# Two attention cores of a fused attention and convolution kernel, each issued from one written-out order: the even value rows first and interleaved with the last logit products, the odd value projections later

## The chip, the cores and the metric

The kernel runs on one core of one Trainium2 chip. The metric is the device time of one execution in microseconds (us). Before the change it was 421.42 us, the median of 3 runs (420.72 to 423.65). Engines are named as in the profile: PE is TensorE (PEld its weight loads), DVE is VectorE, ACT is ScalarE, POOL is GpSimd, SP is SyncE, which only issues transfers.

## What is computed

Two layers alternate, A, B, A, B, with the same weights both times. A is a layer norm, an attention over 8 earlier positions two apart, an output projection and a residual. B is a layer norm, a long convolution with a kernel K that depends on the weights alone, and a residual. There are 2048 positions, 512 channels and 32 heads of 16.

```python
def _A_ref(x, wqkv, wo):
    H = 32; Dh = D // H
    W, dil = 8, 2
    q, k, v = ...                       # x @ wqkv, by heads
    idx = pos[:, None] - (jnp.arange(W) * dil)[None, :]
    mask = idx >= 0
    logits = jnp.einsum("bhsd,bhswd->bhsw", q, kg) * scale      # kg, vg: k, v gathered at idx
    attn = _softmax(jnp.where(mask, logits, -1e9), axis=-1)
    o = jnp.einsum("bhsw,bhswd->bhsd", attn, vg)
    return o @ wo
def _B_ref(u, A_re, ...):
    K = jnp.einsum("dn,dnl,dn->dl", Cc, P, dB).real
    y = irfft(rfft(u) * rfft(K))        # padded to twice the length, along positions
    return y + u * Dskip
x = x + _A_ref(_layernorm(x), wqkv, wo)
x = x + _B_ref(_layernorm(x), ...)      # and both once more
```

## The kernel before, in words

**Layout and stages.** A position is 16 p + a: p is the partition (128), a the "row" (16 rows). A step of two positions back is a step of two rows back at the same p, and, where it leaves the 16 rows, the row 16 further on of the partition before. So keys (`kT_ext`) and values (`v_ext`) are stored with 14 extra rows in front, which are the last 14 rows moved by one partition. For values that move is done by DMA. The even extra rows come from the even rows only and the odd from the odd. All data stays in on-chip memory, in bf16, between the layers.

The program goes through five stages: making K and the front of attention 0 (normalize, transpose, keys, queries), attention core 0, the transform of layer B with the front of attention 1 after it, attention core 1, and the second transform. Only the two attention cores, which are one function, `LayerA.core`, are touched.

**What an attention core does.** It has 4 blocks q of 4 rows, and 4 feature groups ft of 128 channels.

- Logit products, `mult(q, ft)` (L295, DVE): queries times the 8 shifted keys, 128x4096. The result, `prod`, has 2 buffers. `lsum(q, ft)` (L302, PE) sums it over the channels of a head with 32 small matmuls into the PSUM tile L of the block (2 buffers); at ft = 3 the mask is added (L285).
- Softmax of a block: `mx` (L365, DVE, the maximum), `sub_exp` (L372 on PE subtracts it, L375 on ACT is the exponential), `recip` (L382 on PE sums, L384 and L386 on ACT make the reciprocal as the exponential of minus a logarithm), `norm_p` (L392, DVE, the weights `attn`).
- Projections on PE, each copied out by ACT: queries of a block, `q_proj` (L185, copy L187, 2 buffers of `qT`), values of a row, `v_proj` (L351, copy L353). When row 14 is done, two DMAs on SP's queue move the even rows into the extra ones (L356, L357), and the load of `wo` follows in core 0; with row 15 the odd ones go. In core 0 the loads of x into `x_sb` (L1359) hang on the same two places.
- Value rows: `pv_mult` (L402, DVE, 128x4096, `pav` with 2 buffers), `pv_sum` (L412, PE, 64 matmuls; its PSUM tile `po` has 1 buffer; ACT copies it to `oT`, L415), `out_proj` (L422 and L424, PE; L430 on ACT evicts it into `x_sb` with the row's sum, L108 takes the sum of squares; rows 12 to 15 use L428).
- Layer norm for the next layer, by blocks of four rows: `u_begin` (L133, L135, L140 on DVE and then a power on POOL, L141, or two ACT steps, L118 and L119), `u_end` (L148, DVE), `u_apply` (L160, DVE, for odd rows, L158, ACT, for even rows). `x_stats` (L101, DVE) is for the last rows.

**What sets the order.** Each of DVE, ACT, PE and SP runs its instructions in the order in which the program issues them. Nothing is moved by a planner in these stages. In `core` that order comes from loops. The first goes over the logit products of blocks 0 to 2; between them a list of projections is dealt out evenly (`per`, `acc`): the queries of block 1 (in core 1 only; in core 0 they are done earlier), six value rows, the queries of block 2, and the other value rows, even rows ahead of odd ones. What is left of the list is issued after the loop. The second loop goes over the 16 value rows in the order 0, 2, 1, 3, 4 and so on, and has the four logit products of block 3 at its steps 1, 3, 5 and 7.

```python
projs += [(v_proj, a) for a in vs[:6]] + [(q_proj, 2, ft) for ft in range(NDT)]
projs += [(v_proj, a) for a in vs[6:]]
...
proj(100)
linit(3)
q_proj(3, 0)
rows = [0, 2, 1, *range(3, NA)]
for n in range(16):
    pv_mult(rows[n])
```

**Hooks.** Other work hangs on steps of these loops by a dictionary of events. In core 0 it is the making of a table g2 for the transform (indices on POOL, four sines on ACT, L700, each followed by a store to `g_dram` on SP, L701), the reading back of K (`k_half_load`, 18 DMAs for each half into `k_rl`, L1264 and L1280), the fix of its first element (`k_half_fix`, L1350, DVE), and eight copies of K into `k_perm` (`k_part`, L1354; even ones on ACT, odd ones on DVE). The sines use the memory of `k_perm` as scratch, so the first copy of K has to wait until the stores of g2 have read it. The table load for the logarithm and exponential and the load of the transform's weights (`load_w2`, L560) are hooked in too. In core 1 the rest of the front's key and query projections is hooked to the first products.

**After the cores.** The transform stages issue from written orders of their own and begin with a PE pass (L756) over the normalized rows, whose results DVE and ACT cast (L745). They are not changed.

Of the kernel before, what the change touches and what calls it, by code (L numbers as in the profile page):

```python
# [20 lines left out]
P = 128  # L21
S = 2048
# [4 lines left out]
NA = 16  # L27
NDT = 4
# [35 lines left out]
u m UA m u m u m u m u u yD yA u m yA m m u u u m yA m yA  # L64
yA m yD yD yA yD yA yA yA yD z01D z03D yA yA z00D z02D z12D z11A z10D z13B
"""

def build_a_consts(tc, nc, cpool, tpool):
    c = {}
# [93 lines left out]
class LayerA:  # L163
# [140 lines left out]
        if ft == NDT - 1:  # L304
            self.mask(q)

    def core(self, x_sb, u, lnp, ev=None, nprod=0):

        tc, nc, lnst, l = self.tc, self.nc, self.lnst, self.layer
        ident, nident = self.c["ident"], self.c["nident"]  # L310
        scale = float(DH) ** -0.5
        xnT = self.xnT
        ev = ev or {}
        if self.ps_l is None:
            self.open_logits()
        st, linit, mult, lsum = self.st, self.linit, self.mult, self.lsum

        def event(key):
            for f in ev.get(key, ()):
                f()  # L320

        with ExitStack() as c2:
            big = c2.enter_context(tc.tile_pool(name=f"a{l}_big", bufs=1, reuse_waits="tile"))
# [24 lines left out]
            def v_proj(a):  # L348
                pp = pq_tile()
                for dt in range(NDT):  # L350
                    nc.tensor.matmul(pp[:], lhsT=xnT[:, dt, a * P:(a + 1) * P],  # L351
                                     rhs=wv[:, dt, :], start=(dt == 0), stop=(dt == NDT - 1))
                nc.scalar.copy(v[:, 14 + a, :].rearrange("p (d h) -> p d h", h=H), pp[:].rearrange("p (h d) -> p d h", h=H))  # L353
                if a >= 14:
                    b = a - 14
                    nc.sync.dma_start(v[1:113, b:14:2, :], v[0:112, 16 + b:30:2, :])  # L356
                    nc.sync.dma_start(v[113:128, b:14:2, :], v[112:127, 16 + b:30:2, :])  # L357
                    if b + l == 0:
                        self.load_wo(big)
                    event(("v", b))  # L360

            def mx(q):
                L = st[q]["L"]
# [88 lines left out]
            def u_apply(a0, rows, eng=None):  # L452
                rstd, nb = lns[a0]
                for a in rows:
# [2 lines left out]

            nc.sync.dma_start(v[0:1, 0:14, :].rearrange("p a (n c) -> p (a n) c", c=64),
                              self.c["zrow"].unsqueeze(1).to_broadcast([1, 112, 64]))
            projs = [(q_proj, 1, ft) for ft in range(NDT)] if 1 not in self.qT else []  # L460
            vs = [*range(0, NA, 2), *range(1, NA, 2)]
            projs += [(v_proj, a) for a in vs[:6]] + [(q_proj, 2, ft) for ft in range(NDT)]
            projs += [(v_proj, a) for a in vs[6:]]
            slots = [(0, ft) for ft in range(nprod, NDT)] + [(q, ft) for q in (1, 2) for ft in range(NDT)]
            free = 2 if l else 0
            lead = 0 if l else 2
            per, acc = (len(projs) - lead) / (len(slots) - free - 0.5), float(lead)

            def proj(n):
                nonlocal acc  # L470
                acc += n
                while acc >= 1 and projs:
                    f, *args = projs.pop(0)
                    f(*args)
                    acc -= 1

            for q, ft in slots:
                if q == 1 and ft == 0 and 1 not in self.qT:
                    while 1 not in self.qT or projs[0][0] is q_proj:
                        proj(1)  # L480
                event(("m", q, ft))
                mult(q, ft)
                event(("q", q, ft))
                if ft == 0:
                    linit(q)
                if q or ft >= free:
                    proj(per)
                if ft == 0 and q > 0:
                    mx(q - 1)
                lsum(q, ft)  # L490
                if ft == 0 and q > 0:
                    proj(0.5)
                    acc -= 0.5
                    sub_exp(q - 1)
                if ft == 2 and q > 0:
                    recip(q - 1)
                if ft == 3 and q > 0:
                    norm_p(q - 1)
            proj(100)
            linit(3)  # L500
            q_proj(3, 0)
            rows = [0, 2, 1, *range(3, NA)]
            for n in range(16):
                pv_mult(rows[n])
                if n in (0, 8):
                    mx(2 + n // 8)
                if n in (2, 10):
                    recip(2 + n // 8)
                if n in (4, 11):
                    norm_p(2 + n // 8)  # L510
                if n in (1, 3, 5, 7):
                    mult(3, n // 2)
                if n in (7, 11, 15):
                    u_begin(n - 7, n - 3, "act", "act" if n > 7 else "pool")
                if n in (8, 12):
                    u_end(n - 8)
                if n in (9, 10, 13, 14):
                    b0 = 0 if n < 11 else 4
                    r0 = b0 + (0 if n in (9, 13) else 2)
                    u_apply(b0, range(r0, r0 + 2))  # L520
                if n == 15:
                    x_stats(12)
                event(("p", n))
                if n in (1, 3, 5):
                    q_proj(3, n // 2 + 1)
                pv_sum(rows[n])
                if n in (0, 8):
                    sub_exp(2 + n // 8)
                if n == 15:
                    x_stats(13)  # L530
                    if l == 1:
                        u_end(8)
                        u_apply(8, range(8, 12), "dve")
                if n > 0:
                    out_proj(rows[n - 1])
                if n in (1, 3, 5, 7):
                    lsum(3, n // 2)
                event(("o", n))
            if l == 0:
                out_proj(15)  # L540
                return {"a": lambda: [u_end(8), u_apply(8, range(8, 12), "pool")], "s": lambda: x_stats(14), "t": lambda: x_stats(15),
# [744 lines left out]
def kernel(  # L1286
# [16 lines left out]
    nc = tc.nc  # L1303
# [57 lines left out]
    with tc.tile_pool(name="ctmp_g2", bufs=1) as g2tmp, tc.manual_schedule(engines=MAN):  # L1361
        gx, gs = build_g2(nc, g2tmp, C["p21"], g2_dram, kp[:].rearrange("p q a r -> p (q a r)"))
        G = lambda f, h: lambda: f(h)
        K = lambda h, j: lambda: k_part(h, j)
        ev = {("v", 0): [lambda: x_load((0,))], ("v", 1): [lambda: x_load((1, 2, 3))], ("o", 1): [lambda: k_half_load(0)], ("o", 2): [G(gs, 0)], 
              ("m", 0, 3): [G(gx, h) for h in range(4)],
              ("p", 3): [G(gs, 1)], ("p", 4): [G(gs, 2)], ("p", 5): [G(gs, 3), lambda: k_half_load(1)], ("o", 5): [lambda: nc.scalar.preload_act_table_set(EXP_LN)],
              ("p", 6): [lambda: k_half_fix(0), K(0, 0)], ("p", 7): [K(0, 1)], ("p", 8): [lambda: la.load_w2(w2_dram), K(0, 2)], ("p", 9): [K(0, 3)],
              ("p", 12): [lambda: k_half_fix(1), K(1, 0)], ("p", 13): [K(1, 1), K(1, 2)], ("p", 14): [K(1, 3)]}
        late = la.core(x_sb, u, lnp, ev, 3)  # L1370
    late["m"] = C["masks"]
    krctx2.close()
    la.close_logits()
# [13 lines left out]
    with tc.manual_schedule(engines=MAN):  # L1387
# [33 lines left out]
        fb.c_ps.close()  # L1421
        fb.c_grp.close()
        krctx.close()
        ev = {("p", 8): [lambda: la.load_w2(w2_dram)]}
        ev["m", 0, 0] = [last(("P", 3, 0), ("P", 3, 1), ("x", 0), ("x", 2), ("P", 3, 2), ("Q", 0, 1), ("e", 0), ("Q", 0, 2))]
        ev["m", 0, 1] = [last(("e", 1), ("e", 2))]
        ev["m", 0, 2] = [last(("e", 3))]
        ev["q", 0, 0] = [last(("P", 3, 3), ("Q", 0, 3))]
        la.core(x_sb, u, lnp, ev)
    la.close_logits()  # L1430

    fb = FftB(tc, nc, C, consts["ident"], w2_dram, g2_dram, kf_dram, x_sb, 1)
# [47 lines left out]
```

## Time and profile before

| what | value |
|---|---|
| median of 3 runs (lowest, highest) | 421.42 us (420.72, 423.65) |
| the profiled execution's own time | 418.89 us |
| its span, and the mean TensorE clock | 417.1 us, 0.991 |
| busy PE, PEld, DVE, ACT, POOL in the span | 320.5, 231.5, 387.9, 321.7, 37.7 us |
| making K, front of attention 0 | 0 to 114.8 us |
| core 0: logit half, value half | 114.8 to 139.9, 139.9 to 196.7 us |
| transform 0, front of attention 1 | 196.7 to 251.0, 251.0 to 276.1 us |
| core 1: logit half, value half | 276.1 to 312.3, 312.3 to 369.4 us |
| transform 1 | 369.4 to 417.0 us |

The stages overlap at their edges; the cuts are where DVE or PE goes over to the next. How to read it: a number in a "busy" column is the time in which the engine worked, and the stretch's length minus it is the time in which it waited. In a timeline a line is the start in us, the duration, engine, source line, operation, output and inputs with their shapes, and in brackets the idle time before it and what ended that. An "x3" after a line counts the operations that the line stands for. Lines are those of the kernel before unless said otherwise. SPq is SP's queue: its rows show the issue of a DMA, and the data land later.

### The profile page before, as it was taken

Reading aid. Unit: us, or ns where it says so; the run is one execution under the profiler, and the core shown is the slowest. Engines: PE = TensorE matmul, PEld = TensorE weight load, DVE = VectorE, ACT = ScalarE, POOL = GpSimd, SP = SyncE. Lnnn points to the kernel's source line nnn. Section 1 sums busy time; section 2 is a strip of 40 time slices with the busy share of each in tenths; the row PEclk is TensorE's granted clock in tenths of the full one; section 3 lists DMA queues with packets and bytes.
Section 4 is the critical chain, followed back from the end, with each engine's and each line's share of the span. In section 5 each row is a group of like instructions: output and inputs, shape, how many; then the busy total and the mean of one; then the engine's idle time right before and its main releaser. Section 6 shows DMA issues by size and latency. Waiting matters only on the chain.

```text
span 417.1 us, 15864 instructions
## 1 busy us (share of the span) xinstructions
PE 320.5 (77%) x7048; PEld 231.5 (55%) x7106; DVE 387.9 (93%) x515; ACT 321.7 (77%) x552; POOL 37.7 (9%) x46
## 2 busy tenths in 40 slices
PE   3000068999999987778998779999998978896885
PEld 2000036667756565556887768555665655566774
DVE  8999999999899999996999969979779999989995
ACT  6999998987445569987999998863555758779972
POOL 3000200000396000000500000000000020000000
PEclk9999998999999999999999999999999999999899
DMA  8940642113014666393226597730043027504506
GB/s 222 383 125 13 73 90 71 33 40 89 14 40 123 179 180 189 99 389 109 70 89 229 217 306 218 231 99 2 3 114 89 5 79 328 156 3 140 168 10 197
DMA packets 62462, 54.36 MB, mean 130 GB/s; under 512 B 33877, under 2 KB 50874, under 8 KB 61114
## 3 DMA queue, kind: packets, MB, share of 16 engines
q1 hardware_dynamic: 62250, 53.22, 42.0%
q8 instruction: 55, 0.90, 0.9%
q10 hardware_dynamic: 144, 0.13, 0.1%
q14 instruction: 13, 0.11, 0.1%
HBM read 30.28 MB, written 13.24 MB: 104 GB/s over the span
## 4 chain that ended last, share of the span: by engine, by line
PE 35%; DVE 21%; ACT 14%; issue 5%; DMA 5%; SPq 3%; DVEq 0%; ACTq 0%
PE pq L351 6%; DVE pav L402 5%; DVE t L805 5%; PE L L302 4%; DVE a1s L745 4%; PE pk L1175 4%; PE pq L185 3%; DVE prod L295 3%; PE pp L242 3%; PE po L412 3%; PE pp L1113 3%; PE pq L424 2%; SPq L1280 2%; DMA w_sb<-w_dram 2%; ACT ub L818 1%
## 5 line engine op out<-in xcount | busy, mean ns | idle before, releaser
L402 DVE TENSOR_TENSOR pav<-attn,v_ext 128x4096 bf16<-128x4096 bf16 x32 | 72.8, 2283 | 0.1
L295 DVE TENSOR_TENSOR prod<-qT,kT_ext 128x4096 bf16<-128x4096 bf16 x29 | 66.0, 2299 | 3.9 <-PE L L302 3.8
L412 PE MATMUL po<-ident,pav 64*128 64x64 bf16 x2048 | 36.3, 190 | 15.1 <-DVE pav L402 7.7
L412 PEld LDWEIGHTS <-pav 64*128 64x128 bf16 x2048 | 32.5, 95 | 26.0 <-DVE pav L402 14.9
L1103 PE MATMUL pt<-ident,x_blk 128*128 128x128 bf16 x64 | 7.0, 260 | 43.4 <-ACT x_blk L158 43.4
L1015 DVE TENSOR_TENSOR A_t<-A_t,pow_t 128x1024 bf16<-128x1024 bf16 (+4 forms) x46 | 38.1, 868 | 0.2
L424 PE MATMUL pq<-wop,oT 128*128 128x512 bf16 x121 | 31.7, 379 | 4.3 <-issue 3.8
L353 ACT CAST v_ext<-pq 128x512 bf16<-128x512 f32 x32 | 18.8, 587 | 19.2 <-PE pq L351 17.5
L818 ACT CAST ub<-pb 128x1024 bf16<-128x1024 f32 x32 | 32.2, 1036 | 1.7 <-DVE t L805 0.8
L763 PE MATMUL pb<-a1s,w_sb 128*128 128x64 bf16 x768 | 28.4, 196 | 6.2 <-ACT a1s L745 2.9
L302 PEld LDWEIGHTS <-prod 128*128 128x128 bf16 x928 | 27.0, 96 | 8.1 <-DVE prod L295 2.5
L1103 PEld LDWEIGHTS <-x_blk 128*128 128x128 bf16 x64 | 5.4, 117 | 46.1 <-ACT x_blk L158 44.4
L745 DVE CAST a1s<-pb 128x1024 bf16<-128x1024 f32 x23 | 27.0, 1215 | 3.9 <-PE pb L756 3.9
L763 PEld LDWEIGHTS <-w_sb 128*128 128x128 bf16 x768 | 25.8, 100 | 8.6 <-issue 6.8
L351 PE MATMUL pq<-wv,xnT 128*128 128x512 bf16 x118 | 29.9, 379 | 0.5
L1113 PE MATMUL pp<-xnT,kT_ext 128*128 128x512 bf16 x87 | 25.0, 406 | 6.2 <-ACT qT L1118 3.3
L302 PE MATMUL L<-ind,prod 128*128 128x8 bf16 x928 | 27.4, 166 | 0.8 <-DVE prod L295 0.6
L415 ACT CAST oT<-po 128x512 bf16<-128x512 f32 x32 | 18.5, 577 | 11.5 <-PE po L412 11.2
L745 ACT CAST a1s<-pb 128x1024 bf16<-128x1024 f32 x25 | 24.9, 1034 | 2.5 <-PE pb L756 2.2
L1175 PEld LDWEIGHTS <-A_t 128*64 128x64 bf16 (+1 forms) x512 | 22.3, 105 | 3.6
L1175 PE MATMUL pk<-B_t,A_t 128*64 128x84 bf16 (+1 forms) x512 | 24.1, 203 | 0.1
L832 PE MATMUL pb<-Wp,t 64*128 64x64 bf16 x512 | 19.4, 192 | 5.9 <-ACT ub L818 2.8
(225 smaller groups left out, 809.8 us busy)
## 6 DMA issues: line engine op xcount, KB each, us to landing
w_sb<-w_dram SPq DMA_DIRECT2D x8, 1024.0 KB, 9.4
w_dram<-w_zero SPq DMA_DIRECT2D x1, 4096.0 KB, 14.8
kf_ring<-kf_dram SPq DMA_DIRECT2D x13, 256.0 KB, 3.7
kf_ring<-kf_dram SPq DMA_DIRECT2D x26, 128.0 KB, 3.6
v_ext<-v_ext SPq DMA_DIRECT2D x4, 784.0 KB, 6.2
x_blk<-in_A_x_dram SPq DMA_DIRECT2D x4, 512.0 KB, 4.1
kT_ext<-in_A_wqkv_dram SPq DMA_DIRECT2D x4, 512.0 KB, 10.1
x_sb<-in_A_x_dram SPq DMA_DIRECT2D x4, 512.0 KB, 5.4
```

Of the source, the lines that this page charges most:

```text
L295: nc.vector.tensor_tensor(pr, self.qT[q][:, ft].unsqueeze(1).to_broadcast([P, W, 4, P]), kap, ALU.mult)
L302: self.nc.tensor.matmul(L[:, al, w, ft * 8:(ft + 1) * 8], lhsT=pr[:, w, al, :], rhs=self.c["ind8"][:], start=(ft == 0 and w == 0 and al % ...
L351: nc.tensor.matmul(pp[:], lhsT=xnT[:, dt, a * P:(a + 1) * P], rhs=wv[:, dt, :], start=(dt == 0), stop=(dt == NDT - 1))
L402: nc.vector.tensor_tensor(pv[:], attn[:, n % 4].unsqueeze(2).to_broadcast([P, W, DH, H]), vap, ALU.mult)
L412: nc.tensor.matmul(po[:, h, 0, ft, :], lhsT=pvf[rows, w, ft * P:(ft + 1) * P], rhs=ident[rows, rows], start=(w == 0 and ft == 0), stop=(w ...
L424: nc.tensor.matmul(pw[:], lhsT=oT[:, ftp, :], rhs=self.wo[:, ftp, :], start=False, stop=(ftp == NDT - 1))
L745: (self.nc.scalar.copy if eng == "act" else self.nc.vector.tensor_copy)(dst, src)
L763: nc.tensor.matmul(p2[:, j, :], lhsT=self.w2[:, ec * EC + j, :], rhs=a1s[:, ec * EC + j, :], start=True, stop=True)
L818: nc.scalar.copy(ub[:], p2)
L1015: return lambda: nc.vector.tensor_tensor(*args)
L1113: nc.tensor.matmul(pps[kind, b, ft][:], lhsT=la.wqk[:, dt, c:c + P], rhs=la.xnT[:, dt, b * 512:(b + 1) * 512], start=(dt == 0), stop=(dt = ...
L1175: nc.tensor.matmul(o, lhsT=lhs, rhs=Bt[:, ri, c * CH + ql].rearrange("p b g -> p (b g)"), start=(not half and j % 4 == 0 and ri == 0), sto ...
```

## The change

Both cores now get a string, one letter for each step, and `core` only walks through it. The letters are m for `mult`, l for `lsum`, q for `q_proj`, v for `v_proj`, x for `mx`, e for `sub_exp`, r for `recip`, n for `norm_p`, P for `pv_mult`, S for `pv_sum`, O for `out_proj`, t for `x_stats`, b, d and a for `u_begin`, `u_end` and `u_apply` (now one row each). Digits and other capitals are the hooks. In core 0, 0 makes the indices of g2, 1 and 6 read back the halves of K, 2 to 5 are the sines with their stores, 7 is the table load, w the weights' load, 8 and 9 are the fixes, A to H the copies of K. In core 1, 0 to 3 are the rest of the front.

Every step of before is still there, once. What differs is the order:

- The value rows go 2, 0, 4, 6, 3, 1, 5, 8, ... in core 0 and 0, 4, 6, 1, 2, 3, 5, 10, ... in core 1. The four logit products of block 3 stand behind 2, 4, 6 and 8 value products, as before (in core 1 behind 2, 3, 6 and 8).
- The projections have places of their own instead of an even spread: even value rows still come ahead of odd ones, and that of row 15 comes after the last logit sum of block 2.
- The steps of softmax and layer norm and the hooks have other neighbours. An output projection can stand ahead of the value sum that it followed, and the row's normalizing is split by rows.

```diff
+CORE0 = """
+vm0vvvlmxvqlqmeqmlvrlvvmmlqvvnmxlvevmlvmrlvvlvnPxqSeqPSm1OlPr2SPq3mOSlPOPSn4OSmq56O7lP8ASOPOmbBS
+lPxCdwSeOPOaSaraPSODPanSbPOd9ESOaaPFSOPHOaSPGbtSOta
+"""
+CORE1 = """
+0mvl12ml3mqmqqqlqlmvxvevlrvmlmvlqmqmlnxqvvvvlevvmmllrmvvvlvnqPxeSPmqSlPrOSOqmPqSOPOlSPmnSlOPPSmO
+SObwPldxOSeaOPaSPraaPSOnbSOPdSaOPSOPaSaaOPbttSdaaaOa
+"""
+ROWS0 = (2, 0, 4, 6, 3, 1, 5, 8, 7, 9, 11, 10, 13, 12, 14, 15)
+ROWS1 = (0, 4, 6, 1, 2, 3, 5, 10, 7, 8, 9, 11, 12, 13, 14, 15)
+VROWS = (*range(0, 16, 2), *range(1, 16, 2))
...
-    def core(self, x_sb, u, lnp, ev=None, nprod=0):
+    def core(self, x_sb, u, lnp, order, ev, nprod=0):
...
-                    event(("v", b))
+                    if ("v", b) in ev:
+                        ev["v", b]()
...
-            for q, ft in slots:
...
-            for n in range(16):
-                pv_mult(rows[n])
...
+            qft = [(q, ft) for q in range(4) for ft in range(NDT)]
+            blocks = [(q,) for q in range(4)]
+            rows = [(a,) for a in (ROWS1 if l else ROWS0)]
+            ops = dict(
+                m=calls(mult, *qft[nprod:]), l=calls(logit(lsum), *qft[nprod:]),
+                q=calls(q_proj, *qft[len(self.qT) * NDT:]), v=calls(v_proj, *((a,) for a in VROWS)),
+                x=calls(mx, *blocks), e=calls(sub_exp, *blocks), r=calls(recip, *blocks), n=calls(norm_p, *blocks),
+                P=calls(pv_mult, *rows), S=calls(pv_sum, *rows), O=calls(out_proj, *rows[:15]), t=calls(x_stats, (12,), (13,)),
+                b=calls(u_begin, (0, 4, "act", "pool"), (4, 8, "act", "act"), (8, 12, "act", "act")),
+                d=calls(u_end, (0,), (4,), (8,)),
+                a=calls(u_apply, *((a0, (a,)) for a0 in (0, 4) for a in range(a0, a0 + 4)), *((8, (a,), "dve") for a in range(8, 12))))
+            ops = {key: iter(f) for key, f in ops.items()}
+            for c in "".join(order.split()):
+                if c in ev:
+                    ev[c]()
+                else:
+                    next(ops[c])()
...
-        late = la.core(x_sb, u, lnp, ev, 3)
+              "0": lambda: [gx(h) for h in range(4)], "1": lambda: k_half_load(0), "6": lambda: k_half_load(1),
+              "2": G(gs, 0), "3": G(gs, 1), "4": G(gs, 2), "5": G(gs, 3),
+              "7": lambda: nc.scalar.preload_act_table_set(EXP_LN), "w": lambda: la.load_w2(w2_dram),
+              "8": lambda: k_half_fix(0), "9": lambda: k_half_fix(1)}
+        ev |= {c: K(i // 4, i % 4) for i, c in enumerate("ABCDEFGH")}
+        late = la.core(x_sb, u, lnp, CORE0, ev, 3)
...
-        la.core(x_sb, u, lnp, ev)
+        la.core(x_sb, u, lnp, CORE1, ev)
```

## The prediction, made before the changed kernel was run

> **What bounds the kernel now.** The page came first: it says which engine has no room left.
>
> ```profile
> PE 320.5 (77%) x7048; PEld 231.5 (55%) x7106; DVE 387.9 (93%) x515; ACT 321.7 (77%) x552; POOL 37.7 (9%) x46
> ```
>
> DVE is busy 387.9 of 417.1 us, so an order can only win idle DVE time. The view by stretches says where it is; its columns are the stretch, its length, then PE, PEld, DVE, ACT busy.
>
> ```profile
> 114.80:139.90 25.10, 24.19 (x348) 14.78 (x350) 23.94 (x13) 12.67 (x23) 17.25 (x11) 1.00 0.40 103
> 139.90:169.60 29.70, 23.88 (x694) 16.61 (x700) 29.32 (x21) 23.39 (x47) 0.51 (x1) 1.00 0.57 165
> ...
> 276.10:312.30 36.20, 35.73 (x483) 21.53 (x490) 31.04 (x19) 19.51 (x35) 0.00 (x0) 1.00 0.13 35
> 312.30:340.90 28.60, 24.57 (x708) 16.92 (x716) 28.53 (x18) 17.46 (x42) 0.00 (x0) 1.00 0.13 35
> ```
>
> Rows 1 and 3 are the logit halves of the two attention cores. PE is full there (35.73 of 36.20), while DVE lacks 5.1 us in core 1 and 1.2 in core 0. Rows 2 and 4 are the starts of the value halves: DVE full, PE with 4 to 6 us of room. DVE's timeline names its waits in core 1:
>
> ```profile
> 288.47 1.23 DVE L365 TENSOR_REDUCE mx<-L 128x128 bf16<-128x1024 f32 x1 [0.61 <-PE L L285]
> 289.61 4.48 DVE L295 TENSOR_TENSOR prod<-qT,kT_ext 128x4096 bf16<-128x4096 bf16 x2
> 294.96 2.29 DVE L295 TENSOR_TENSOR prod<-qT,kT_ext 128x4096 bf16<-128x4096 bf16 x1 [0.87 <-PE L L302]
> 298.55 0.69 DVE L392 TENSOR_TENSOR attn<-ex,rs 128x1024 bf16<-128x1024 bf16 x1 [1.29 <-ACT rs L386]
> ```
>
> The last one ends after a chain: logit sums, sum of exponentials on PE, two ACT steps, then the attention weights. It comes again at 311.69.
>
> Third, SyncE's timeline, as nothing on it may be late:
>
> ```profile
> 140.99 0.64 SPq L356 DMA_DIRECT2D v_ext<-v_ext  x1
> ...
> 142.62 4.42 SPq L1359 DMA_DIRECT2D x_sb<-in_A_x_dram  x3
> 147.09 0.61 SPq L1264 DMA_DIRECT2D k_rl<-kd_dram  x1
> 147.74 12.15 SPq L1280 DMA_DIRECT2D k_rl<-kd_dram  x17
> 159.99 3.83 SPq L701 DMA_DIRECT2D g_dram<-k_perm  x4
> ```
>
> From 140.99, when the last value projection (row 15) is copied out, the queue runs without a pause to the stores of g2 at 159.99. The tile view of g_dram gives 5.1 us from issue to landing: the first store lands at 165.1. ScalarE's first copy into that memory (L1354) starts at 166.90.
>
> [...] the trace agrees that all products cost alike (2.28 us, one each 2.20 us), so no order makes one cheaper. [...]
>
> ```profile
> 169.09 1.02 POOL L141 TENSOR_TENSOR ln_rstd<-ln_rstd,ln_mh 128x4 f32<-128x4 f32 x1 [37.05 <-DVE ln_rstd L140]
> ...
> 341.19 2.89 POOL L141 TENSOR_TENSOR ln_rstd<-ln_rstd,ln_mh 128x4 f32<-128x4 f32 x1 [96.59 <-DVE ln_rstd L140]
> ```
>
> It is the same power on 128x4. In core 0 it began before a value product and took 1.02; in core 1 a product was running from 340.92 to 343.20, and it ended at 344.08, 0.9 after that.
>
> **The change part by part.** Nothing is removed or added: all products, projections, sums, copies and DMAs are the same, and each queue's DMAs keep their order. What moves is worked out by lanes, with one instruction's pitch: logit product or value product 2.20 (DVE), maximum 1.13, attention weights 0.60; projection 0.87, logit sum 0.80, value sum 1.04, output projection 1.08 (PE); projection copy 0.48, row statistics with eviction 1.36, K copy 0.95 (ACT).
>
> *Core 0, logit half.* From 114.87 on DVE has 9 products (19.8), 2 maxima (2.3) and 2 weights (1.2) before the first value product: 138.2 if it never waits. It now starts at 139.91. The new order puts each weights step behind the next product, so the waits of 0.37 and 0.72 and the small ones between products go: lead 1.7. PE's sum doesn't change: from 118.56, 16 projections, 8 logit sums and 2.3 for the rest are 22.6, so 141.2, as now (the next projection, q3, starts at 141.30). So DVE leads only where PE has room later, and it has (row 2). But the projection of row 15 now stands behind the last logit sum and mask, 1.0 us later on PE; its copy ends at 141.8 instead of 140.97, and everything queued behind it on SyncE moves by 0.8: the odd shift, the three x_sb loads, 18 loads of k_rl, the g2 stores. The shift itself is safe: the new row order needs odd rows first after four even ones, at about 152.6, and it lands at about 148.5.
>
> *Core 0, value half.* DVE runs on: 8 value products, 4 logit products, a maximum, a weights step and the K fix are 28.3, so 166.5, when the first layer-norm block (L133) is due; now it starts at 168.47. This lead is given back. ScalarE reaches its first K copy at about 163.4 (now 165.6 before its table load), but the first g2 store lands at 165.1 + 0.8 = 165.9. Behind that copy stand, in ScalarE's order, the evictions of rows 5 and 1, and the block needs row 1's statistics: 165.9 + 0.95 + 0.48 + 1.36 = 168.7. Row 1 was long done before; this is a new wait of about 2 us on DVE. With 0.2 for the last scalars and 0.6 for the K copy behind them the next value product starts at about 169.8; now 169.56. From there DVE has 22.0 us to the end of its last one (now 22.3; one apply of 0.33 has moved behind): 191.8 against 191.9.
>
> *Core 0, end.* Now an output projection stands ahead of the last value sum, which starts 0.85 after its product. In the new order it is done before, and the first 16 K transform matmuls (L756) stand ahead too. So value sum 191.9 to 193.0, copy to 193.6, two output projections to 195.1; now 196.05. The transform stage starts 0.95 earlier and keeps it: ScalarE (52.79 of 54.30) and DVE (50.27) are full in it. Core 0: minus 1.0.
>
> *Core 1, logit half.* PE is full in both orders. Walking both lanes: the first product of block 1 now waits for a logit sum behind three more projections (287.1, about 1.3 idle), two further products wait 1.3 and 0.8, but both weights steps (1.29 each) are covered. The first value product starts at 310.7; now 312.30. Lead 1.6. It needs the even shift, which landed at 309.99 and whose projection keeps its place on PE: 0.7 of slack. PE's first value sum stays at about 315.0 (now 314.65), and its room in row 4 carries the lead.
>
> *Core 1, value half.* The layer-norm block comes at 338.9 (now 340.46). It now has one value product behind it before its result is read, where product and maximum stood before. The power on GpSimd [...] ends 0.9 later, as in the row above; DVE then stands for about 0.9 and the maximum is late with it. Bounds: 0 if the power slips in ahead, 1.0. I take 0.9. The end is as now, 0.7 earlier. Later transfers follow: the w2 load waits for the last logit product and moves with it.
>
> Sum: 1.0 + 0.7 = 1.7; I round up to 2.0, since the first DVE cast of the transform gains more than PE does (now idle for 2.56 before it). The profiled run took 418.89 around its span of 417.1; the median shown is 421.42, and the difference applies to it: 419.4.
>
> **Rivals.**
> 1. *Both leads kept.* ScalarE isn't held at the K copy (if the k_rl loads run faster than the sum says) and the power slips in. Then core 0 gives 2.8 (P-sums end at 190.1) and core 1 1.6: 4.4, so 417.0. For: DVE has no other wait in the value halves. Against: the queue has no pause in which to catch up.
> 2. *Hidden.* The leads arrive and the transform stages don't pass them on, as they wait for transfers or for GpSimd's applies (POOL, 198.20 to 204.94): 421.4. For: ScalarE and DVE share that stage, and it has a store chain of its own (L791, L808). Against: those transfers start from the same casts.
> 3. *Slower.* The wait at the K copy is longer than the lead: each us by which row 15's copy is later than 0.8 holds ScalarE, then row 1's statistics, then DVE, one for one. It decides from 0.8 + 2.0 = 2.8 us on; at 5 us the time is 423.6. For: PE in this stretch has under 1 us of room, so any hitch lands on the row 15 projection, last in its line. Against: the same matmuls in sum.
> That the change does nothing is out: the order on each engine differs.
>
> **How the numbers follow.** Forecast 0.45 (418 to 421), rival 1 0.20, rival 2 0.20, rival 3 0.15. The range 416.2 to 423.6 leaves out the ends of rivals 1 and 3. About 1% (4.2 us) is what a measurement can tell from no change. Faster by over 1% (under 417.2) takes most of rival 1 and a little of the forecast: 0.18. Slower by over 1% (over 425.6): 0.07, of rival 3. The rest, 0.75, is within 1%.
>
> **What would show it.** Right: first value product of core 0 near 138.2; SyncE's odd shift near 141.8; about 2 us of DVE idle before L133 or L135 of core 0 that ACT ends; about 0.9 before L148 of core 1 that POOL ends; core 1's weights steps without a wait. Wrong: no wait at L133 (rival 1), new DVE idle in the transforms (rival 2), a shift after 143 (rival 3).

## The result and the profile after

The changed kernel took 421.86 us (median of 20 runs, 417.47 to 423.92), the kernel before 421.42 (20 runs, 419.21 to 424.05). The ratio is 1.0006 with a 95% interval of 0.9982 to 1.0030, that is +0.3 us (-0.8 to +1.3): no difference that can be measured. The ratios of all runs here leave out executions over 1.5% above the fastest of their kernel (five of 22 for the later K copy below, at most three in any other set). The profiled execution took 420.96 us around a span of 419.2.

Lines of the changed kernel: L308 logit product, L401 weights, L411 value product, L421 value sum, L431 and L433 output projection, L439 and L121 eviction and sum of squares, L146 and L148 layer-norm block, L154 POOL's power, L161 scalars, L364 shift, L374 maximum, L1222 and L1238 loads of K, L1312 copies of K, L659 stores of g2, L703 casts of the transform, L790 its later matmuls. Times are us.

| mark | before | predicted | after |
|---|---|---|---|
| core 0: first value product | 139.91 | 138.2 | 139.15 |
| SyncE: odd shift | 140.99 | 141.8 | 142.74 |
| value product behind the layer-norm block | 169.56 | 169.8 | 170.50 |
| end of the last value product | 191.9 | 191.8 | 193.0 |
| last output projection done | 196.05 | 195.1 | 197.8 |
| tenth DVE cast of transform 0 into `a1s` | 209.91 | | 211.13 |
| core 1: first logit product | 276.15 | | 279.24 |
| from it to the first value product | 36.15 | 34.55 | 34.56 |
| from it to the first cast of transform 1 | 93.31 | 92.6 | 92.30 |
| span | 417.1 | 415.1 | 419.2 |

So the span's 2.1 is +1.2 up to transform 0, +1.9 in it and in the front behind it, and -1.0 in core 1. The view by stretches of the changed kernel (stretch, length, PE, PEld, DVE, ACT, POOL busy):

```profile
114.80:139.90 25.10, 23.88 (x348) 14.47 (x347) 24.95 (x14) 12.08 (x22) 19.25 (x11) 1.00 0.41 103
139.90:169.60 29.70, 25.32 (x644) 15.95 (x642) 27.95 (x17) 23.76 (x47) 0.00 (x0) 0.99 0.57 163
276.10:312.30 36.20, 36.20 (x492) 21.63 (x491) 31.61 (x23) 19.53 (x35) 0.00 (x0) 1.00 0.18 47
312.30:340.90 28.60, 26.91 (x714) 17.43 (x712) 28.60 (x16) 18.20 (x43) 0.00 (x0) 1.00 0.13 36
```

In core 0 DVE's waits have moved: 0.15 left in the logit half (1.2 before), 1.75 in the start of the value half (0.4 before). DVE's timeline there, and ScalarE's:

```profile
165.50 2.27 DVE L308 TENSOR_TENSOR prod<-qT,kT_ext 128x4096 bf16<-128x4096 bf16 x1
168.90 0.16 DVE L146 SCALAR_TENSOR_TENSOR ln_msq<-ln_s 128x4 f32<-128x4 f32 x1 [1.13 <-ACT x_sb L439]
169.59 0.16 DVE L148 SCALAR_TENSOR_TENSOR ln_veps<-ln_s,ln_msq 128x4 f32<-128x4 f32 x1 [0.52 <-ACT ln_junk L121]
...
170.50 2.29 DVE L411 TENSOR_TENSOR pav<-attn,v_ext 128x4096 bf16<-128x4096 bf16 x1
```

```profile
166.68 1.04 ACT L1312 COPY k_perm<-k_rl 128x1024 bf16<-128x1024 bf16 x1 [1.27 <-DMA g_dram<-k_perm]
```

This is the predicted chain: the K copy waits for the store of g2, row 1's statistics are behind it, and DVE waits for those, 1.65 in all. SyncE's timeline shows why the store is late: the odd shift is 1.75 later than before, and the stores 2.6.

```profile
142.74 0.64 SPq L364 DMA_DIRECT2D v_ext<-v_ext  x1
...
148.29 14.22 SPq L1238 DMA_DIRECT2D k_rl<-kd_dram  x17
162.61 2.66 SPq L659 DMA_DIRECT2D g_dram<-k_perm  x4
```

In core 1 the weights steps no longer wait (two of 1.29 before), and the new wait for POOL has the predicted size. DVE's timeline:

```profile
302.79 0.69 DVE L401 TENSOR_TENSOR attn<-ex,rs 128x1024 bf16<-128x1024 bf16 x1
...
313.20 0.69 DVE L401 TENSOR_TENSOR attn<-ex,rs 128x1024 bf16<-128x1024 bf16 x1
313.80 2.29 DVE L411 TENSOR_TENSOR pav<-attn,v_ext 128x4096 bf16<-128x4096 bf16 x1
...
345.69 0.16 DVE L161 SCALAR_TENSOR_TENSOR ln_nb<-ln_s,ln_rstd 128x4 f32<-128x4 f32 x1 [0.91 <-POOL ln_rstd L154]
```

What the prediction had nowhere stands in PE's timeline. "issue" means that nothing that the profile records was waited for:

```profile
152.50 1.00 PE L421 MATMUL po<-ident,pav 64*128 64x64 bf16 x57
154.37 0.27 PE L421 MATMUL po<-ident,pav 64*128 64x64 bf16 x7 [0.87 <-issue]
...
194.51 1.11 PE L421 MATMUL po<-ident,pav 64*128 64x64 bf16 x64 [0.25 <-ACT oT L424]
...
251.45 0.21 PE L790 MATMUL pb<-Wp,t 64*128 64x64 bf16 x2 [1.62 <-issue]
```

PE stops in the middle of the value sum of row 6, between its 57th and 58th matmul, and once more in the transform. From here on a stop is a standstill of PE that is marked "issue". (The line at 194.51 is the last value sum of core 0, to which the account below comes back.) The kernel before has stops too, but none between 149 and 158:

```profile
188.50 0.76 PE L412 MATMUL po<-ident,pav 64*128 64x64 bf16 x40 [0.92 <-issue]
```

These stops have a candidate in the table of DMA queues on the page:

```profile
q8 instruction: 55, 0.90, 0.9%
```

55 packets of 16 KB are 0.90 MB. PE's 7106 matmuls and 7106 weight loads are the only stream of that size (DVE has 515 instructions, ScalarE 552). That the pieces are PE's program is an estimate from these counts: some 258 instructions to a piece. The order of the matmuls bears it out. Counted through the whole trace, the five stops of 0.2 or more marked "issue" from 150 to 256 stand ahead of matmuls 1500, 2140, 2268, 3804 and 3932. These lie multiples of 128 matmuls apart, which with their weight loads is 256 instructions. At most borders PE doesn't stand that long: the whole trace has these five stops, of 0.26 to 1.62, beside 55 pieces. A stop there would be a piece that came late.

### The profile page after: what moved, and what is told of

Its sections match the earlier page's. It is cut to its first block, busy times and chain, and to the rows that moved or that the text cites. A ratio compares the mean times of both kernels' runs of the same rounds, so it can differ in the third digit from the quotient of the medians.

```text
span 419.2 us, 15928 instructions
## 1 busy us (share of the span) xinstructions
PE 326.5 (78%) x7106; PEld 230.5 (55%) x7106; DVE 388.1 (93%) x515; ACT 322.0 (77%) x552; POOL 39.8 (9%) x46
## 4 chain that ended last, share of the span: by engine, by line
PE 37%; DVE 21%; ACT 10%; issue 8%; DMA 6%; SPq 2%; POOLq 1%; DVEq 0%; ACTq 0%
PE pk L1133 5%; DVE t L763 5%; PE pq L359 5%; DVE pav L411 4%; PE pp L1071 4%; DVE prod L308 4%; PE L L315 4%; DVE a1s L703 3%; PE pp L255 3%; PE pq L198 3%; DMA w_sb<-w_dram 2%; ACT ub L776 1%; PE po L421 1%; SPq L1238 1%; PE pb L721 1%
## 5 line engine op out<-in xcount | busy, mean ns | idle before, releaser
L411 DVE TENSOR_TENSOR pav<-attn,v_ext 128x4096 bf16<-128x4096 bf16 x32 | 72.6, 2284 | 0.0
L308 DVE TENSOR_TENSOR prod<-qT,kT_ext 128x4096 bf16<-128x4096 bf16 x29 | 66.1, 2301 | 5.3 <-PE L L315 3.4
L421 PEld LDWEIGHTS <-pav 64*128 64x128 bf16 x2048 | 33.1, 96 | 22.6 <-DVE pav L411 11.6
L421 PE MATMUL po<-ident,pav 64*128 64x64 bf16 x2048 | 37.1, 192 | 10.5 <-DVE pav L411 3.4
L433 PE MATMUL pq<-wop,oT 128*128 128x512 bf16 x128 | 33.4, 383 | 2.5 <-ACT oT L424 2.5
L1071 PE MATMUL pp<-xnT,kT_ext 128*128 128x512 bf16 x96 | 26.2, 401 | 6.0 <-ACT qT L1076 3.1
L359 PE MATMUL pq<-wv,xnT 128*128 128x512 bf16 x128 | 30.9, 379 | 0.0
L703 DVE CAST a1s<-pb 128x1024 bf16<-128x1024 f32 x23 | 27.0, 1217 | 2.6 <-PE pb L714 2.6
L703 ACT CAST a1s<-pb 128x1024 bf16<-128x1024 f32 x25 | 24.9, 1036 | 1.8 <-PE pb L714 1.5
L790 PE MATMUL pb<-Wp,t 64*128 64x64 bf16 x512 | 19.2, 191 | 7.2 <-ACT ub L776 2.8
L198 PE MATMUL pq<-xnT,kT_ext 128*128 128x512 bf16 x96 | 23.8, 380 | 0.0
```

What stands on the lines that cost most here:

```text
L198: nc.tensor.matmul(pq[:], lhsT=self.wqk[:, dt, ft * P:(ft + 1) * P], rhs=self.xnT[:, dt, q * 512:(q + 1) * 512], start=(dt == 0), stop=(dt ...
L308: nc.vector.tensor_tensor(pr, self.qT[q][:, ft].unsqueeze(1).to_broadcast([P, W, 4, P]), kap, ALU.mult)
L411: nc.vector.tensor_tensor(pv[:], attn[:, n % 4].unsqueeze(2).to_broadcast([P, W, DH, H]), vap, ALU.mult)
L421: nc.tensor.matmul(po[:, h, 0, ft, :], lhsT=pvf[rows, w, ft * P:(ft + 1) * P], rhs=ident[rows, rows], start=(w == 0 and ft == 0), stop=(w ...
L703: (self.nc.scalar.copy if eng == "act" else self.nc.vector.tensor_copy)(dst, src)
L1071: nc.tensor.matmul(pps[kind, b, ft][:], lhsT=la.wqk[:, dt, c:c + P], rhs=la.xnT[:, dt, b * 512:(b + 1) * 512], start=(dt == 0), stop=(dt = ...
```

## The experiments

First theory (A): core 0 loses at the K copy and in its tail, core 1 wins. Rival (C): nothing but spread. The first four runs take the cores apart and undo one suspected cost each.

**New order in core 0 only.**

```diff
+CORE1 = <the order of before, as letters>;  ROWS1 = (0, 2, 1, 3, 4, ... 15)
```

> Core 0 in the new order, core 1 in the old. Theory A (core 0's order loses its lead at the K copy on ScalarE and then on PE, core 1's order gains): slower than before by 1.0 to 1.8 us, so about 422.8 against 421.4; in the trace DVE again waits 1.2 to 2.0 us before the first layer-norm block of core 0, the second DVE cast of the transform starts near 199.7 (198.55 before), and core 1 takes the same time as before from its first product to the first cast of the second transform (93.3 us). Theory B (core 0's order is neutral, and the 1.62 us in which PE stood without a recorded cause near 251 in the changed kernel's trace makes the difference): equal to before wherever that standstill is absent. Theory C (both orders equal, run variation only): same as before.

Measured: 1.0047 of before (1.0022 to 1.0072), +2.0 us. Slower, so C falls. B (core 0 neutral, the stop near 251 makes the difference) falls too, as this profile has no stop there. But the trace is not A's. PE's timeline and DVE's:

```profile
152.53 1.00 PE L421 MATMUL po<-ident,pav 64*128 64x64 bf16 x57
155.31 0.37 PE L421 MATMUL po<-ident,pav 64*128 64x64 bf16 x7 [1.77 <-issue]
```

```profile
170.96 0.16 DVE L146 SCALAR_TENSOR_TENSOR ln_msq<-ln_s 128x4 f32<-128x4 f32 x1 [2.88 <-ACT x_sb L439]
171.65 0.17 DVE L148 SCALAR_TENSOR_TENSOR ln_veps<-ln_s,ln_msq 128x4 f32<-128x4 f32 x1 [0.52 <-ACT ln_junk L121]
```

DVE waits 3.40 in place of 1.65, and ScalarE's K copy, at 168.74, waits for nothing (0.01): ScalarE itself is late, since PE stood for 1.77 at the same 57th matmul. PE's matmuls also took double time behind that stop (four of a projection 1.91 at 156.86, a value sum 1.89 at 158.71; in the changed kernel's profile 1.02 and 1.11, at a granted clock of 1.00 from 155 to 165), so the 3.40 isn't the stop's alone.

**New order in core 1 only.**

```diff
+CORE0 = <the order of before, as letters>;  ROWS0 = (0, 2, 1, 3, 4, ... 15)
```

> Core 0 in the old order, core 1 in the new. Theory A: faster than before by about 1.0 us (420.4 against 421.4): from the first product of core 1 to the first cast of the second transform 92.3 us, where before has 93.3; POOL again ends a wait of 0.9 us before the scalars L161. No standstill of PE over 1 us near 251. Theory C: same as before.

Measured: 0.9973 (0.9947 to 0.9999), -1.1 us, and 92.29 us between the two marks, as expected. PE's waits in the transforms show no "issue" above 0.7, as expected too. The longest standstill of the first transform (1.85, at 246.05) is of another kind, a wait for a product of DVE, which had waited for a DMA (in the line: us in total, times, longest):

```profile
PE pb L790 <- DVE t L763: 2.9, 4, 1.9
```

So this run doesn't say whether the stop near 251 belongs to the change.

**First K copy later.**

```diff
-...8ASOPOmbBS...
+...8SOPOAmbBS...
```

> The changed kernel with one letter of core 0 moved: ScalarE's first copy of K stands behind the evictions of rows 1 and 5. Theory A (that copy, waiting for the first store of g2, holds row 1's statistics): the waits of 1.13 and 0.52 us before the layer-norm block disappear, the next value product starts near 168.9 (170.50 in the changed kernel), and the time falls by 1.0 to 1.6 us, to about 420.5. Rival (DVE would have waited for something else, or PE's tail sets the end of core 0): the waits move elsewhere and the time falls by less than 0.4 us.

Measured: 0.9979 (0.9952 to 1.0006), which doesn't tell it from the changed kernel, nor from the 1.0 to 1.6 us that A expected. The trace does: the waits before the layer-norm block stayed, at 0.82 and 0.52, and the next value product began at 170.48. Here PE had stood for 1.58 at the 57th matmul, and ScalarE came to row 1's eviction only at 168.09. So the waits don't hang on the copy alone, and A falls as the whole cause. The copy's own share stays open.

**Maximum first, in core 1.**

```diff
-...bwPldxOSe...
+...bwPlxdOSe...
```

> The changed kernel with two letters of core 1 exchanged: the maximum of block 3 before the scalars that need POOL's power. Theory A: the wait of 0.91 us for POOL goes, the maximum starts 0.9 us earlier, and the time falls by 0.9 us, to about 421.0. Rival (PE or ScalarE sets the pace behind it): the time falls by less than 0.3 us, and a wait for PE appears before a later value product.

Measured: 1.0014 (0.9981 to 1.0047), no gain. DVE's and PE's timelines of this run:

```profile
348.50 1.22 DVE L374 TENSOR_REDUCE mx<-L 128x128 bf16<-128x1024 f32 x1
349.63 0.15 DVE L161 SCALAR_TENSOR_TENSOR ln_nb<-ln_s,ln_rstd 128x4 f32<-128x4 f32 x1
```

```profile
359.96 0.39 PE L433 MATMUL pq<-wop,oT 128*128 128x512 bf16 x1 [0.64 <-issue]
...
364.51 0.26 PE L421 MATMUL po<-ident,pav 64*128 64x64 bf16 x6 [0.98 <-issue]
```

The POOL wait is gone and the last value product ends 1.0 earlier relative to the core's first product (84.40, 85.40 in the changed kernel), but PE stands at two piece borders near the end, 1.62 in all (0.17 in the changed kernel), and the core is only 0.35 shorter. In core 0, in the same order as the changed kernel's, PE stood for 2.50 at the 57th matmul. Over four profiles with this order of PE that stop was 0.87, 1.58, 1.77 and 2.50: the spot is fixed, the length is not.

From here on theory F: PE's instruction pieces come late because they share the DMA engines with the data that the later shift has moved to 143 to 153 us.

**All x loads early.**

```diff
-("v", 0): lambda: x_load((0,)), ("v", 1): lambda: x_load((1, 2, 3)),
+("v", 0): lambda: x_load((0, 1, 2, 3)),
```

> The changed kernel with all four loads of x into x_sb at the first place (behind the even shift, when the queue is empty), none behind the odd shift. Theory F (in core 0 PE's own instruction pieces of 16 KB arrive behind the data that the late odd shift and the x loads put on the DMA engines; PE then stands inside the value sum of row 6, at its 57th of 64 matmuls, for 0.87 to 2.5 us, and everything after it is late): the standstill falls below 0.5 us, the stores of g2 issue about 3 us earlier and ScalarE's first K copy doesn't wait for them; the wait before the first layer-norm block falls below 0.5 us, and the time is 1.5 to 2.5 us below that of the changed kernel, about 419.7 beside 421.2 of before. Theory A (only the K copy is held): the standstill stays, the wait falls by the 1.3 us of the K copy. Rival (ScalarE is simply full there): waits stay at 1.5 to 3.4 us, and the time falls by less than 0.5 us.

Measured: 0.9968 (0.9951 to 0.9986), -1.3 us against before, 1.6 below the changed kernel. PE's, SyncE's and DVE's timelines:

```profile
152.42 1.11 PE L421 MATMUL po<-ident,pav 64*128 64x64 bf16 x64
```

```profile
146.43 10.84 SPq L1238 DMA_DIRECT2D k_rl<-kd_dram  x17
157.37 4.93 SPq L659 DMA_DIRECT2D g_dram<-k_perm  x4
```

```profile
167.62 0.14 DVE L146 SCALAR_TENSOR_TENSOR ln_msq<-ln_s 128x4 f32<-128x4 f32 x1
```

No stop in row 6's sum, stores 5 us earlier, no wait before the block. The DMA view in stretches of 2.5 us finds the piece. First the changed kernel, 151 to 153.5 (in 148 to 150.5, at 99.9% data, it shows none); then this run, 148 to 150.5 (packets, MB, share of the engines):

```profile
q1 hardware_dynamic: 499, 0.64, 98.4%
q8 instruction: 1, 0.02, 2.3%
```

```profile
q1 hardware_dynamic: 326, 0.14, 30.8%
q8 instruction: 1, 0.02, 3.4%
```

With the engines 30.8% full the piece comes over 1.4 us earlier than with them full: this run has none in 151 to 153.5, where data take 8.8%, and in the changed kernel's packet records it starts at 151.92, takes 0.93, and PE goes on at 154.37, 1.5 after its end. None of the five profiles with early loads and no added copies (this one and four below) has the stop. F holds so far.

The time needs a caution: the new core 0 is now level with the old one (0.9968 beside the 0.9973 of the new order in core 1 alone). The early loads take away the loss, but the gain forecast for core 0 doesn't appear.

**The same with core 0 in the old order.**

```diff
+CORE0, ROWS0 as before; x loads as in the run above
```

> Core 0 in the old order, core 1 in the new, and all x loads at the first place. Theory F: the old order of core 0 has no standstill of PE over 0.3 us between 150 and 157, so the early loads give it nothing: within 0.5 us of the kernel with the new order in core 1 alone (0.9973 of before). Rival (the early loads help by themselves, whatever the order): 1 us or more below that.

Measured: 1.0044 (1.0021 to 1.0067): 3.0 us above the run with the new order in core 1 alone. Both expectations were wrong, and DVE's timeline says why:

```profile
150.14 4.49 DVE L411 TENSOR_TENSOR pav<-attn,v_ext 128x4096 bf16<-128x4096 bf16 x2 [2.30 <-DMA v_ext<-v_ext]
```

The early loads hold up the odd shift behind them, and the old order needs it for its third row, which waits 2.30 for it here (in the profile of before, with late loads, the shift's second DMA lands at 147.71, 6.0 after its issue, and that row begins at 147.84). The new order takes four even rows first and has room. So early loads cost 3.0 in the old order of core 0 and win 1.6 in the new one. The run exchanges the whole order of core 0; that the row order in it decides is read from this wait.

**Piece borders moved.**

```diff
+spare = pst.tile([P, 4, P], BF16, name="pt")
+for k in range(64):
+    nc.tensor.transpose(spare[:, k % 4, :], raw["C_im"][:, k % 4, :], ident[:])
```

> The changed kernel with 64 transposes more on PE (128 instructions, into a tile that nobody reads) at 8 us, where PE stands for 42 us anyway. They take no time of the path but move the borders of all later instruction pieces by half a piece. Theory F: the standstill without a recorded cause in core 0 isn't at the 57th matmul of row 6's value sum any more, but 128 PE instructions earlier in the order (the query projection and the output projection ahead of it, near 151.2), and that near 251 leaves its matmul too. Rival (the standstill belongs to that matmul, which waits for something the profile doesn't name): it stays at the 57th of row 6. The time may go either way, by up to 1.5 us.

Measured: 1.0079 (1.0035 to 1.0123). PE's timeline:

```profile
152.38 1.11 PE L421 MATMUL po<-ident,pav 64*128 64x64 bf16 x64
```

The stop left the 57th matmul, so it isn't that matmul's own. It didn't show 128 instructions earlier either. The stops that this profile has lie where F puts them: 1.11 at 185.32, 0.55 at 194.43 and 2.27 at 251.73 stand ahead of matmuls 2268, 2524 and 4060, the same grid of 128 as before, though the work has moved on by 64 matmuls. So the stop near 251 left its matmul too. Its last value product of core 0 ended at 191.41 (193.00 in the changed kernel), with the x loads as late as there: without the stop, a late queue alone didn't make core 0 late. Why this kernel is 3 us slower stays open; in its profile the loss comes behind core 0, from the tenth cast of transform 0 to core 1 (69.93 in place of 68.11).

**Early x loads and the later K copy.**

```diff
 x loads as above
-...8ASOPOmbBS...
+...8SOPOAmbBS...
```

> Early x loads, and ScalarE's first K copy behind the evictions of rows 1 and 5 as well. Theory F: a further 0.5 to 1 us below early x loads alone, as the copy (0.95) no longer stands ahead of row 1's statistics; no wait over 0.3 us before the first layer-norm block; about 419. Rival (with early x loads the copy is no longer in the way): equal to early x loads alone within 0.4 us.

Measured: 0.9985 (0.9967 to 1.0004), 0.7 us above early loads alone, which the runs don't tell apart. In both profiles DVE doesn't wait at the block: once the store is early, the copy is in nobody's way.

**Traffic that nobody waits for.**

```diff
 x loads early, and at ("v", 1):
+for b in (1, 2, 3):
+    nc.sync.dma_start(spare[b], x_v[:, b * 4:(b + 1) * 4, :])   # DRAM to DRAM
```

> Early x loads, and at the odd shift three copies of 512 KB from memory to memory that nobody reads, in the place that the x loads had in the changed kernel. Theory F (data on the DMA engines holds up PE's instruction pieces): the standstill without a recorded cause at the 57th matmul of row 6's value sum comes back (0.8 us or more, against none with early x loads), the stores of g2 issue near 162 again (157.4), and the time is 1 to 2.5 us above early x loads alone. Rival (the x loads mattered by what waits for them, and not as traffic): no standstill there, and the time within 0.5 us of early x loads alone.

Measured: 1.0012 (0.9990 to 1.0034), 1.9 us above early loads alone, whose interval it doesn't touch. PE's timeline:

```profile
152.33 1.00 PE L421 MATMUL po<-ident,pav 64*128 64x64 bf16 x57
155.12 0.27 PE L421 MATMUL po<-ident,pav 64*128 64x64 bf16 x7 [1.79 <-issue]
```

The stop is back at its matmul, the piece lies in 151 to 153.5 again, where data take 88.1% of the engines, and DVE waits 2.03 and 0.52 before the block. These copies also push the stores of g2 to 163.66, but ScalarE's K copy, at 167.41, waits for nothing, and DVE has no wait between 138 and 166: what is late is PE, and ScalarE behind it. F is shown for the stop. In the five profiles with early loads alone the last value product of core 0 ended at 191.7 to 193.3, in the five with the stop at 192.5 to 197.1; how the time divides between the stop and the double times behind it (1.91 at 156.53 here) isn't shown.

**Standstill split.** In the run with early loads PE waited 2.03 for a value product at 171.12 and then ran at half rate for some 5 us (a value sum took 1.89 in place of 1.11, four projection matmuls 1.91 in place of 1.03). Its last value product ended at 193.30, no earlier than the changed kernel's 193.00: in this profile the lead was lost again. Theory G: the standstill causes the half rate.

```diff
 x loads early
-...P8ASOPOmbBSlPx...
+...P8ASOPmbBSlOPx...
```

> Early x loads, and in core 0 the output projection of row 5 behind the last logit sum instead of ahead of the value sum of row 8. In the run with early x loads PE stood for 2.03 us there, its matmuls then took twice as long (value sum 1.89 instead of 1.11, four projection matmuls 1.91 instead of 1.03) for about 5 us, and DVE waited 1.37 and 0.96 us behind it. Theory G (PE standing for about 2 us lowers its rate): the standstill is split into 0.6 and 1.5 us, no matmul group behind it takes double time, DVE's waits of 1.37 and 0.96 go, and the time falls by 1.5 to 2 us below early x loads alone, to about 417.5 beside 420.4 of before (0.993). Rival (the double time has another cause, for instance a clock granted lower in that stretch in any case): double times and waits stay, and the time is the same within 0.5 us.

Measured: 0.9945 (0.9925 to 0.9965), -2.3 us: the lowest here, below both kernels. It isn't told apart from early loads alone, nor from the new order in core 1 alone. PE's timeline:

```profile
163.07 1.46 PE L421 MATMUL po<-ident,pav 64*128 64x64 bf16 x64 [1.24 <-DVE pav L411]
164.46 0.61 PE L431 MATMUL pq<-x_sb,ident 128*128 128x512 bf16 x1
164.86 1.91 PE L433 MATMUL pq<-wop,oT 128*128 128x512 bf16 x4
```

Double times again, behind a standstill of 1.24 that had no such effect in the run with early loads alone.

> The same, and in core 1 the maximum of block 3 before the scalars that wait for POOL. In the changed kernel this exchange won 1.0 us at its place and lost 0.65 of it again, where PE's instruction pieces came late near the end of the core. If that loss depends on the order, 0.3 us below the run with the split standstill; if it was chance, 1.0 us below.

This adds the exchange in core 1 to it. Measured: 0.9960 (0.9941 to 0.9978), no gain, though core 1 is 0.6 shorter in its profile. Double times again (1.85 at 168.84), behind nothing longer than 0.65.

**Standstill filled.**

```diff
 x loads early
+z=calls(lambda n: self.warm(pq_tile(), n, self.wo[:, 0, :]), (8,)),
-...bBSlPx...
+...bBSlzPx...
```

> Early x loads, and 8 matmuls of 128x512 into a tile that nobody reads between the last logit sum of core 0 and the value sum behind it, where PE stood for 2.03 us in the run with early x loads alone. The order of all other work is that of early x loads alone. Theory G (standing still lowers PE's rate): PE stands for under 0.5 us there, no group of matmuls between 162 and 182 takes double time, DVE's waits of 1.37 and 0.96 us go, and the time is 1 to 2 us below early x loads alone, about 0.993 of before. Rival (double time comes by itself, whatever PE does; the run with the split standstill had one behind 1.24 us only, and the run with the exchange in core 1 one behind 0.65): a stretch of double time again, and no gain within 0.7 us of early x loads alone (0.9968).

Measured: 0.9961 (0.9937 to 0.9985), as early loads alone. The granted clock (third number from the right) in stretches of 5 us, first early loads alone, then with the filler:

```profile
165.00:170.00 5.00, 3.76 (x105) 2.35 (x102) 4.66 (x7) 4.94 (x12) 1.02 (x1) 1.00 0.15 39
170.00:175.00 5.00, 3.88 (x69) 2.47 (x70) 5.00 (x6) 1.60 (x3) 0.00 (x0) 0.50 0.40 110
```

```profile
165.00:170.00 5.00, 5.00 (x102) 2.77 (x101) 4.25 (x7) 4.06 (x11) 1.02 (x1) 0.76 0.12 28
170.00:175.00 5.00, 5.00 (x92) 2.81 (x90) 5.00 (x5) 2.87 (x5) 0.00 (x0) 1.00 0.44 118
```

The low clock is elsewhere, not gone. G isn't shown.

## Why the prediction was right and wrong

The time lies in the range and within 1% of before, as forecast. The likeliest value, 419.4, came from a sum of which one half held. The gain of core 1 and an unforeseen loss of core 0 cancel, so that the time fell into the range is in part luck.

- **Core 1, logit half: right.** Lead 1.6 predicted, 1.59 measured.
- **Core 1, value half: right.** The wait for POOL's power was 0.91 (0.9): the power took 2.89, from 342.77, and ended 0.88 after the value product that ran beside it; in core 0 it took 1.02. The kernel before has the same 2.89 and 1.02; that the product is what lengthens it was not tried. The core gave 1.0 in the trace and 1.1 (0.0 to 2.2) in the runs, for 0.7.
- **Core 0, logit half: right in kind, too large.** Of the lead of 1.7, 0.76 came. From 114.76 nine products, two maxima and two weights steps give 138.02, and 139.15 was measured. 0.42 of the difference is one product of 2.70 (at 124.71). The kernel before has the same (at 124.82): the prediction took it for small waits that would go. 0.41 is a weights step (from 129.53 to 130.54), and 0.26 comes at a later product, 0.15 of it a wait for a copy of ScalarE. POOL was at its g2 indices until 134, busy for 19.25 in this stretch (17.25 before). Two of its L654 steps took 1.38 at 112.53, where DVE stood from 112.68 on, and 8.67 at 121.42, beside DVE's products. I gave no price to the two running side by side. That it is this fits, but wasn't tried.
- **SyncE's lateness: right in kind, too small.** 1.75 in place of 0.8: the row 15 projection was done on PE at 141.93, where the sum has 141.2 (PE waited 0.58 for a maximum).
- **Core 0, value half: the step that failed.** "DVE runs on" to 166.5 and then waits about 2 was near for the profiled run (1.65), but 3.40 in two others of the same order. I priced the late queue only by what waits for its data ("The shift itself is safe"). Its traffic also delays PE's instructions, which wait in no queue of the program: PE stops for 0.87 to 2.50, ScalarE and row 1's statistics follow.
- **Core 0, end: wrong.** I expected 0.95, since a projection stands ahead of the last value sum. But PE has no gap above 0.25 from 189.6 to 197.8, so what is put ahead pushes the sums back: the last sum starts 1.5 after its product has ended (0.85 before), and the end came at 197.8, 1.8 later than before. This is read from the one trace; no run tried another order there. Core 0 was to give 1.0 and cost 2.0 (0.9 to 3.0).
- **Transform 0.** "Keeps it" overlooked that this stage varies: from its tenth DVE cast to core 1's first product the 14 profiles have 66.1 to 69.9, and the shown one of before, 66.24, is near the bottom. PE's stop near 251 in the changed kernel (1.62) is part of that.

Of the rivals, "hidden" has the number and not the cause: core 0 brought no lead that a transform could have hidden. "Slower" has the right chain for core 0, by another start.

Open: the order's own part in the low clock (0.88 and 0.78 at 165 to 175 in the changed kernel, 1.00 before; but the profile with the old order of core 0 and the new one of core 1 has a mean clock of 0.982, below the changed kernel's 0.990), why core 0 gains nothing even without the stop, and the 3 us lost with the moved borders.

## What to carry to other kernels

A DMA queue that runs late is priced by two things: who waits for the data, and what else is on the DMA engines when an engine with many small instructions needs its next piece of program (here 0.87 to 2.50 us of PE at one border). Look for stops marked "issue" in the middle of a run of equal matmuls, and for the instruction queue's packets beside full data engines. A reorder that wins nothing can still make room: here taking even rows first left the odd shift time, so that moving loads ahead of it won 1.6 us where it had cost 3.0. The sum of both is still no measured gain over leaving core 0 as it was (0.9968 beside 0.9973; 0.9945 with one projection moved as well, which the runs don't tell apart).

## What the runs showed of the hardware

- The profile's instruction queue q8 brings 55 packets of 16 KB, counted with the data on the core's 16 DMA engines. By the counts above they are PE's program, 256 instructions to a piece; that is an estimate from this kernel's traces. With data on the engines for 99.9% of 148 to 150.5 in the changed kernel, PE stood for 0.87 us at the border behind, and for 1.58 to 2.50 in three more profiles with this order of PE. With the x loads moved out of that stretch (30.8%) it didn't stand there (five profiles), and it stood for 1.79 with copies of 1.5 MB that nobody reads put in their place (88.1% in 151 to 153.5; 98.4% in the changed kernel, 8.8% with early loads alone). At most other borders it didn't stand for 0.2 or more.
- In the clock records of these traces TensorE's granted clock falls to 0.5 for 3.41 or 6.83 us at a time in core 0: at 168.76 in the changed kernel, just behind a standstill of 2.52, at 170.03 in a standstill of 2.03 (early loads), at 163.62 behind one of 1.24 (one projection moved), and at 168.90 in a run that had stood for no longer than 0.65 in the 4 us ahead (the exchange in core 1 added). What brings it isn't shown.
